# Two early blocks of a squared-ReLU feed-forward kernel put together: first products first, then seven quarter products over chunks 2 to 5

## The chip, the cores and the metric

The kernel runs on one core of one Trainium2 chip. The metric is the device time of one execution in microseconds (us); the kernel before took 207.84 us, the median of three runs (207.48 to 207.92). A core has five engines that each work off their own instruction stream in program order: TensorE (PE, matrix products, with its weight loads shown as PEld), VectorE (DVE), ScalarE (ACT), GpSimd (POOL) and SyncE (SP, here only an issuer of DMAs). An instruction that waits for another engine's result holds back everything behind it on its own engine.

## The reference

A retention recurrence with one decay per head, followed by a two-layer feed-forward with a squared ReLU:

```python
# q, k, v: (4, 8, 768, 64) fp32; w_in: (512, 2048); w_out: (2048, 512)
for t in range(S):
    state = gamma[None, :, None, None] * state + einsum('bhd,bhe->bhde', k[:, :, t], v[:, :, t])
    y[:, :, t] = scale * einsum('bhd,bhde->bhe', q[:, :, t], state)
x = y.transpose(0, 2, 1, 3).reshape(3072, 512)
h = maximum(x @ w_in, 0)
out = (h * h) @ w_out
```

The output is 3072 x 512 in fp32; the products are made in bf16.

## The kernel before, in words

**Tiles.** The 3072 tokens are 24 chunks of 128 (six to a batch entry). For each chunk an "attention" part makes `xt`, the transposed 512 x 128 input of the feed-forward: scale q and k (DVE), bring v to bf16 in `v_bd` (POOL), transpose q and k on PE and copy them out of PSUM (`qT`, `k_bd`, ACT), score products on PE (two halves, each with four 128-wide matmuls into the single PSUM buffer `st`), masking of each half into `pt` (DVE), a state product and its copy `s_bd`, the output products `y` (PE), and a copy of `y` into `xt` (ACT). Chunks 0 to 3 are done in pairs at the start, chunks 4 to 7 by `attend`, chunks 8 to 23 in a packed form by `attend2`, whose transposes are DMAs.

**Blocks.** The feed-forward goes over blocks of chunks, `BLOCKS = [4, 2, 2, ...]`: block 0 is chunks 0 to 3, block 1 chunks 4 and 5, block 2 chunks 6 and 7. The first product of a block (x @ w_in) fills a PSUM bank `psf` of 128 x 512 by four groups of matmuls or more; ACT takes it out with a ReLU into `h` (`relu`, L779) and DVE squares it in place (L750). Four `psf` banks rotate. The second product (h @ w_out) comes in two forms. Blocks 0 and 1 use the plain form (`second`, L966): 16 matmuls of 512 columns for a chunk, then ACT copies the bank to `osb` and SP stores it. Blocks 2 to 10 (`SEVEN`) use seven quarter products (`seven_products`, L785 to 901): the two chunks of a block and the two halves of w_out are taken as 2 x 2 blocks, and seven products of 8 matmuls with 256 columns (L804) take the place of eight; this needs sums of parts of `h` on DVE (`first_sums`, s3, s4, L800), and four sums of parts of w_out (`sum_w_out`, L303, 8 instructions in the whole kernel).

**Order.** The order of work is written out by hand. The feed-forward is cut into pieces, each about 0.87 us of PE work: 12 pieces for block 0's first product (one 128-row slice f = 4 to 15 of `h` each; f = 0 to 3 are done before), 16 for its second, 8 for block 1's first product, 8 for its second, and so on. After each piece a counter n goes up by one, starting with 5 after the first, and `before(n)` issues whatever was `put` at place n: parts of the attention of a later chunk, casts of weights, loads. Then `take_squares` issues the squares that are due. So a place is a position in every engine's stream. A pipeline step at place n stands on PE between piece n and piece n + 1.

**Around the change.** SP's stream starts with q, k, v of chunks 0 to 3, then the four quarters of w_in (1 MB each; each is cast to bf16 by DVE, ACT and POOL, `cast_w`), then q, k and v of chunk 4, then chunks 5, 6, 7 as their places come. POOL loads w_out with a cast in the DMA (`load_w_out`, L159) at places 7, 11, 15 and 19. Chunk 4's attention lies at places 21 to 31, chunk 5's at 28 to 35, chunk 6's at 30 to 42, chunk 7's at 40 to 49. At places 35 to 44 DVE clears ten parts of tiles for the packed form (`zero_off_diagonal`, L342). Pools that matter here: `stage` has 4 buffers (w_in's quarters, then k and v of whole batches), `opool` has 4 (`osb`), `ps_st` has 1.

Of the kernel before, what the change touches and what calls it, by code (L numbers as in the profile page):

```python
# [25 lines left out]


SEVEN = range(2, 11)
# [3 lines left out]
def kernel(  # L32
# [55 lines left out]
    def load_q(m):  # L88

        b, i = chunks[m]  # L90
        t = ldqpool.tile([P, H, 2, D], FP32, name="qn")
        src = q[b, :, i * C : (i + 2) * C, :].rearrange("h (s r) d -> s h r d", r=2)
        nc.sync.dma_start(t[:], src)
        raw_q[m] = t
# [11 lines left out]
    def load_kv(m):  # L106
        b, i = chunks[m]
        for name, src, to in (("kn", k, raw_k), ("vn", v, raw_v)):
            if m % 2 == 0:
                kv_tiles[name] = ldpool.tile([P, 2 * H * D], FP32, name=name)  # L110
            t = kv_tiles[name].rearrange("s (c h d) -> s c h d", c=2, h=H)[:, m % 2]
            nc.sync.dma_start(t, src[b, :, i * C : (i + 1) * C, :].rearrange("h s d -> s h d"))
            to[m] = t

    def load(m):
        if m % 2 == 0:
            load_q(m)
        load_kv(m)

    def stage_tile(size):  # L120
        t = stage.tile([P, 2 * NCH * NPAIR * D], FP32, name="stage")
        return t[:, 0:size]

    def batch_loads(m, name, size):
# [4 lines left out]
        t = stage_tile(2 * NCH * NPAIR * D)  # L129
# [38 lines left out]
    for g in range(1, NQ):  # L168
        load_w_in(g)
# [171 lines left out]
    def zero_off_diagonal(t, hh):  # L341
        nc.vector.memset(t[halves[hh], :, 1 - hh, :], 0.0)  # L342
# [12 lines left out]
    def scale_kv(m):  # L355
        b, i = chunks[m]
        ks = kspool.tile([P, H, D], BF16, name="ks")
        scale(nc.vector, ks, raw_k.pop(m), kf[:, i])
        v_bd = v_bds[m % 2]
# [4 lines left out]
        at[m].update(ks=ks, v_bd=v_bd)  # L364
# [378 lines left out]

    def take_squares():
        while squares:
            hv, on_scalar = squares.pop(0)
            if on_scalar:
                nc.scalar.activation(hv, hv, AF.Square)  # L748
            else:
                nc.vector.tensor_mul(hv, hv, hv)  # L750
# [27 lines left out]
    def relu(hv, hp, on_scalar=False):  # L778
        nc.scalar.activation(hv, hp[:], AF.Relu)  # L779
        squares.append((hv, on_scalar))  # L780
# [124 lines left out]
    def first_unit(tb, g, c, parts=(0, 1)):  # L905
# [11 lines left out]
        if 1 in parts:  # L917
            relu(h_of(tb, g * FPQ, (g + 1) * FPQ)[:, :, cols], open_ps.pop((tb, g, c)))

    def ffn_pieces(tb):  # L920
# [8 lines left out]
        elif tb <= 2:  # L929

            for c in range(nch):
                for g in range(NQ):
                    first_unit(tb, g, c)
                    if tb in SEVEN and (c, g) == (1, 3):
                        first_sums, rest = seven_products(tb)
                        first_sums(slice(0, 4))
                    yield
            if tb in SEVEN:
                yield from rest()
                return  # L940
        else:
            h_tiles(tb)
            per = 512 // TB
            if tb in SEVEN:
                first_sums, rest = seven_products(tb)
            for f0 in range(0, NFB, per):
# [3 lines left out]
                relu(h_of(tb, f0, f0 + per), hp, tb in SEVEN and f0 // per in (1, 3))  # L950
# [4 lines left out]
                if f0 // per == 5 and tb in SEVEN:  # L955
                    first_sums(slice(0, 4))
                yield
            if tb in SEVEN:
                yield from rest()
                return  # L960


        def second(op, j, g, cols=slice(0, DM)):
            for fq in range(FPQ):
                f = g * FPQ + fq
                nc.tensor.matmul(  # L966
                    op[:],
                    lhsT=h_of(tb, f)[:, 0, j * C : (j + 1) * C],
                    rhs=w_out_bf[g][:, fq, cols],
                    start=(f == 0),  # L970
                    stop=(f == NFB - 1),
                )

        def store(op, j, cols=slice(0, DM)):
            osb = opool.tile([P, DM], FP32, name="osb")
            nc.scalar.activation(osb[:, cols], op[:], AF.Copy)
            r0 = (first[tb] + j) * C
            nc.sync.dma_start(out[r0 : r0 + C, cols], osb[:, cols])


        together = nch if tb == 0 else 1
        for j0 in range(0, nch, together):
# [187 lines left out]
```

## Time and profile before

| | before |
|---|---|
| median of 3 runs | 207.84 us (207.48 to 207.92) |
| profiled execution, time | 208.11 us |
| its span, first to last instruction | 206.3 us |
| granted TensorE clock, mean over the span | 0.992 |
| PE / PEld / DVE / ACT / POOL busy | 197.0 / 160.4 / 151.4 / 132.5 / 64.3 us |
| ReLU of a 128 x 512 bank on ACT (L779) | 96 of 595 ns |
| square of 128 x 512 on DVE (L750) / on ACT (L748) | 80 of 475 ns / 16 of 630 ns |
| second product, plain, 512 columns (L966) | 96 matmuls |

How to read it: the profile is one execution, whose time outside the span is 208.11 - 206.3 = 1.8 us. Matmuls are pipelined and their listed length holds the time in the array, so the rate of PE is better read from the chain of waits, where eight matmuls in a row stand with the time that they add. Busy time of an engine counts no waits. In the timeline a row merges instructions of one kind that follow one another ("x8"), the first column is the start, the second the time from the start of the first to the end of the last, and brackets give idle time in front of the row and what ended it.

### The profile page before, as it was taken

The page shows a single profiled execution, that of the slowest core. Times are in us where ns is not written, and L with a number is a line of the kernel's source. Part 1 is how long each engine was busy: PE and PEld are TensorE (multiplying, and loading weights), DVE is VectorE, ACT ScalarE, POOL GpSimd, SP SyncE. Part 2 cuts the span into 40 slices and gives each one's busy share as a digit, 9 for nine tenths or more (in the row PEclk, how much of TensorE's full clock was granted, in tenths as well). Part 3 has the DMA queues.
Part 4 walks back from the last instruction along what each step waited for, and adds up shares of the span by engine and source line. Part 5 has one row for each costly group of instructions (what it writes and reads, how often), then busy time and mean ns, then how long its engine had stood idle before and what let it go on. Part 6 is the DMA issues. An engine that isn't in the chain of part 4 may idle for free.

```text
span 206.3 us, 5736 instructions
## 1 busy us (share of the span) xinstructions
PE 197.0 (95%) x2325; PEld 160.4 (78%) x2325; DVE 151.4 (73%) x304; ACT 132.5 (64%) x267; POOL 64.3 (31%) x122
## 2 busy tenths in 40 slices
PE   5698999999999999999999999999999999999993
PEld 1467644457975898988989999999988989998882
DVE  4777896538796899579588697797796797484373
ACT  8365884147945585792795794784776776864720
POOL 5332654011210441462245235252226226100000
PEclk9889999999999999999999999999999999999999
DMA  6999999999999978999999999998868952400202
GB/s 160 290 313 379 365 213 208 197 249 265 289 184 135 289 132 124 214 220 215 132 227 152 200 242 170 201 221 186 155 188 161 242 104 31 128 3 1 104 0 102
DMA packets 92730, 38.12 MB, mean 185 GB/s; under 512 B 68512, under 2 KB 88224, under 8 KB 92704
## 3 DMA queue, kind: packets, MB, share of 16 engines
q1 hardware_dynamic: 90592, 35.66, 82.2%
q0 software_dynamic: 2112, 2.10, 6.3%
q8 instruction: 18, 0.29, 0.7%
q14 instruction: 8, 0.07, 0.1%
HBM read 27.26 MB, written 6.29 MB: 163 GB/s over the span
## 4 chain that ended last, share of the span: by engine, by line
PE 79%; DVE 8%; ACT 5%; DMA 4%; issue 3%; POOL 0%; DVEq 0%
PE psf L770 36%; PE psf L804 13%; PE tp L804 9%; PE psf L966 8%; DMA qn<-in_q_dram 2%; DVE h L750 2%; DMA kT<-ks_bdp 2%; PE st L671 2%; PE y L727 2%; PE y L720 1%; PE c_ps L698 1%; ACT h L779 1%; ACT k_bd L395 1%; PE y L326 1%; DVE pt L558 1%
## 5 line engine op out<-in xcount | busy, mean ns | idle before, releaser
L770 PE MATMUL psf<-xt,w_in_bf 128*128 128x256 bf16 (+2 forms) x880 | 91.9, 259 | 0.2 <-ACT xt L498 0.2
L770 PEld LDWEIGHTS <-w_in_bf 128*128 128x128 bf16 x880 | 71.1, 98 | 11.6 <-issue 0.3
L779 ACT ACTIVATE h<-psf 128x512 bf16<-128x512 f32 x96 | 56.2, 595 | 17.3 <-PE psf L770 16.6
L750 DVE TENSOR_TENSOR h<-h 128x512 bf16<-128x512 bf16 x80 | 36.6, 475 | 16.1 <-ACT h L779 15.5
L632 POOL CAST ks_bdp<-stage 64x512 bf16<-64x512 f32 x32 | 24.9, 777 | 41.5 <-issue 24.4
L649 POOL COPY v_bd<-v 64x512 bf16<-64x512 bf16 x32 | 20.6, 644 | 39.1 <-DVE v L641 38.0
L804 PEld LDWEIGHTS <-h 128*128 128x128 bf16 x288 | 26.2, 98 | 4.0 <-DVE h L750 1.2
L800 DVE TENSOR_TENSOR osb<-psf,u 128x256 f32<-128x256 f32 x34 | 13.7, 422 | 17.2 <-ACT u L845 10.0
L966 PE MATMUL psf<-w_out_bf,h 128*128 128x512 bf16 x96 | 22.5, 379 | 0.0
L345 DVE TENSOR_TENSOR qs<-qn,qf 128x512 bf16<-128x512 f32 x22 | 17.7, 816 | 1.5 <-DMA qn<-in_q_dram 1.5
L734 ACT ACTIVATE xt<-y 128x512 bf16<-128x512 f32 x16 | 12.0, 747 | 8.8 <-PE y L727 8.8
L966 PEld LDWEIGHTS <-h 128*128 128x128 bf16 x96 | 8.9, 98 | 9.0
L804 PEld LDWEIGHTS <-k_bd 128*128 128x128 bf16 x144 | 13.8, 98 | 1.5
L707 ACT ACTIVATE s_bd<-c_ps 64x256 bf16<-64x256 f32 x29 | 10.6, 367 | 3.6 <-PE c_ps L698 3.6
L641 DVE TENSOR_TENSOR v<-stage,kf 128x512 bf16<-128x512 f32 x16 | 12.6, 786 | 0.0
L678 DVE TENSOR_TENSOR pt<-st,cmask 128x512 bf16<-128x512 f32 x16 | 11.0, 687 | 0.9 <-PE st L671 0.5
L804 PE MATMUL tp<-w_out_bf,h 128*128 128x256 bf16 x72 | 11.2, 273 | 0.2 <-DVE h L750 0.2
L708 ACT ACTIVATE s_bd<-c_ps 64x256 bf16<-64x256 f32 x29 | 11.0, 378 | 0.4
L800 DVE TENSOR_TENSOR k_bd<-h 128x512 bf16<-128x512 bf16 x18 | 10.7, 597 | 0.3
L421 DVE TENSOR_TENSOR pt<-st,cmask 128x512 bf16<-128x512 f32 x8 | 5.5, 689 | 7.4 <-PE st L414 7.4
L804 PE MATMUL psf<-w_sum,h 128*128 128x256 bf16 x72 | 10.8, 273 | 0.0
L748 ACT ACTIVATE h<-h 128x512 bf16<-128x512 bf16 x16 | 10.1, 630 | 0.5
(129 smaller groups left out, 277.5 us busy)
## 6 DMA issues: line engine op xcount, KB each, us to landing
qn<-in_q_dram SPq DMA_DIRECT2D x12, 512.0 KB, 5.1
out_dram<-osb SPq DMA_DIRECT2D x23, 256.0 KB, 3.5
stage<-in_moe_w_in_dram SPq DMA_DIRECT2D x3, 1024.0 KB, 11.9
stage<-in_k_dram SPq DMA_DIRECT2D x32, 96.0 KB, 4.1
stage<-in_v_dram SPq DMA_DIRECT2D x32, 96.0 KB, 4.0
w_out_bf<-in_moe_w_out_dram POOLq DMA_DIRECT2D x4, 512.0 KB, 10.5
kn<-in_k_dram SPq DMA_DIRECT2D x2, 512.0 KB, 6.4
vn<-in_v_dram SPq DMA_DIRECT2D x2, 512.0 KB, 7.2
```

Source lines behind the costliest of these rows:

```text
L345: engine.tensor_tensor(out=out, in0=by, in1=table[:, :, None].to_broadcast([P, H, D]), op=ALU.mult)
L632: nc.gpsimd.tensor_copy(ks[rows, :, hh, :].rearrange("s (u p) d -> s u p d", u=2), kn[rows])
L641: nc.vector.tensor_tensor(out=v2.rearrange("s (u p) d -> s u p d", u=2), in0=vn, in1=kf2[:, i, :, :, None].to_broadcast([P, 2, NPAIR, D]), ...
L649: nc.gpsimd.tensor_copy(v_bd[rows, :, hh, :], v2[rows])
L678: nc.vector.tensor_tensor(out=pt[:], in0=st[:], in1=cmask2.rearrange("s r t -> s (r t)")[:, None, :].to_broadcast([P, 2 * NPAIR, C // 2]), ...
L734: nc.scalar.activation(xts[tb][:, :, off : off + C].rearrange("e p (s r) -> e p r s", r=2), y[:], AF.Copy,)
L750: nc.vector.tensor_mul(hv, hv, hv)
L770: nc.tensor.matmul(hp, lhsT=w_in_bf[g][:, cb, fq * 128 : (fq + 1) * 128], rhs=xts[tb][:, cb, cols], start=(cb == 0), stop=(cb == NCB - 1),)
L779: nc.scalar.activation(hv, hp[:], AF.Relu)
L800: nc.vector.tensor_tensor(out=out, in0=in0, in1=in1, op=op)
L804: nc.tensor.matmul(to, lhsT=left[:, j], rhs=right(j) if callable(right) else right[:, j], start=(start and j == 0), stop=(stop and j == NF ...
L966: nc.tensor.matmul(op[:], lhsT=h_of(tb, f)[:, 0, j * C : (j + 1) * C], rhs=w_out_bf[g][:, fq, cols], start=(f == 0), stop=(f == NFB - 1),)
```

## The change

The first product of block 1 (chunks 4 and 5) is moved in front of block 0's second product. Chunks 0 and 1 keep the plain second product, as 8 pieces of four matmuls for two chunks in turn. Chunks 2 and 3 (called x below) and chunks 4 and 5 (y) get seven quarter products, interleaved by hand in one list (`early_pieces`, 112 matmuls of 256 columns, a piece for each 7 of them). The places are counted as before: 5 to 16 block 0's first product, 17 to 24 block 1's, 25 to 32 the plain product, 33 to 48 the seven products; from 49 on block 2 as before.

With it move: the attention of chunks 4 and 5 (places 8 to 19), 6 and 7 (31 to 44); the loads (q and k of chunk 4 in front of the last quarter of w_in, which is split in two; v of chunk 4 and k, v of chunk 5 behind it; chunks 6 and 7 as five DMAs from POOL's queue at place 20; w_out at 13, 14, 16, 17); the sums of w_out (25 to 31). Block 1's squares are held back and done on ACT at places 25 to 32. The sums of `h` for x (8 instructions of 512 columns, places 18 to 24) and for y (4 of 1024 columns, places 33 to 36) write a scratch tile from `stage`, which later becomes the tile of the k loads of chunk 12 on. The ten clears go to POOL.

```diff
-        nc.vector.memset(t[halves[hh], :, 1 - hh, :], 0.0)
+        nc.gpsimd.memset(t[halves[hh], :, 1 - hh, :], 0.0)
...
-    for g in range(1, NQ):
-        load_w_in(g)
+    load_w_in(1)
+    load_w_in(2)
+    load_q(4)
+    load_kv(4, "k")
+    load_w_in(3, parts=2)
+    load_kv(4, "v")
+    load_kv(5, "k")
+    load_kv(5, "v")
...
+    def late_square(on_scalar):
+        square(late_squares.pop(0)[0], on_scalar)
...
+        def p1(e):
+            e.oa, e.ob = (opool.tile([P, DM], FP32, name="osb") for _ in range(2))
+            yield from product(e, "pa", e.left(0, 0), w[0, 0], True)
+            copy(e.oa[:, lo], e.pa)
+        def p2(e):
+            yield from product(e, "pb", e.left(0, 1), w[1, 0], True)
+            add(e.oa[:, lo], e.pb)
+        def p6(e):
+            yield from product(e, "pa", of(e.s[1]), of(t2), False)
+            copy(e.oa[:, hi], e.pa)
+        def p5(e):
+            yield from product(e, "pd", of(e.s[0]), of(t1), True)
...
+        def c22(e):
+            add(e.ob[:, hi], e.pd)
+            nc.sync.dma_start(out[e.r0 + C : e.r0 + 2 * C], e.ob[:])
+            return ()
+        def p3(e):
+            yield from product(e, "pd", of(e.s[2]), w[1, 1], False)
+            add(e.oa[:, hi], e.pd)
+            nc.sync.dma_start(out[e.r0 : e.r0 + C], e.oa[:])
+        order = [
+            (p1, x), (p1, y), (p2, x), (p6, x), (p6, y), (p5, x), (p7, x), (p7, y), (p4, x),
+            (c22, x), (p4, y), (p3, x), (p5, y), (p2, y), (c22, y), (p3, y),
+        ]
...
+    def attend(m, q_at, qturn_at, k_at, v_at, turn_at, scores_at, state_at, outputs_at):
...
     put(6, cast_w, "in", 2)
-    for g, place in enumerate((7, 11, 15, 19)):
+    put(11, cast_w, "in", 3, (0,))
+    put(13, cast_w, "in", 3, (1,))
+    attend(4, (8, 9), 10, 9, 13, 11, (12, 13), 14, 15)
+    attend(5, None, None, 15, 17, 16, (17, 18), 18, 19)
+    for place, g in zip((13, 14, 16, 17), range(NQ)):
         put(place, load_w_out, g)
-    for m, place in ((5, 10), (6, 14), (7, 18)):
-        put(place, load, m)
-    put(10, cast_w, "in", 3)
-    for half, at_places in enumerate(((25, 25, 25, 25), (31, 31, 48, 48))):
+    put(20, load_q, 6, nc.gpsimd)
+    for m, name in ((6, "k"), (6, "v"), (7, "k"), (7, "v")):
+        put(20, load_kv, m, name, nc.gpsimd)
+    attend(6, (31, 32), 34, 32, 33, 35, (36, 37), 38, 40)
+    attend(7, None, None, 36, 38, 38, (40, 41), 41, 44)
+    early_at(0, 2, 0, 18, (18, 19, 20, 21, 21, 22, 23, 24))
+    for half, at_places in enumerate(((25, 25, 26, 26), (29, 30, 30, 31))):
...
-    attend(4, 21, (23, 25, 27, 29, 31))
-    attend(5, None, (28, 30, 32, 33, 35))
-    attend(6, 30, (33, 35, 37, 39, 42))
-    attend(7, None, (40, 42, 44, 46, 49))
+    for place in range(25, 33):
+        put(place, late_square, True)
+    early_at(1, 0, 3, 32, (33, 33, 34, 36))
     packed = pack_constants()
     put(27, next, packed)
     put(34, next, packed)
...
-        (12, "k"): [47, 48, 49, 50, 52, 53, 55, 56] + [74 + j for j in range(8)],
+        (12, "k"): [49, 50, 51, 52, 53, 54, 55, 56] + [74 + j for j in range(8)],
...
+    def pieces():
+        yield from first_pieces(0)
+        yield from first_pieces(1)
+        yield from plain_pieces(0, range(2))
+        yield from early_pieces((0, 1))
+        for tb in range(2, len(BLOCKS)):
+            yield from first_pieces(tb)
+            yield from rests[tb]()
```

In `early_pieces`, p7 and p4 are like p6 (bank `pa` goes on accumulating and is copied to a quarter of `ob` by ACT each time); p2, c22 and p3 add a bank onto the copied quarter on DVE (128 x 256). x and y have one bank each for `pa`, `pb` and `pd`. The arguments of `attend` are the places of: the two scalings of q, the transposes of q, the scaling of k, the cast of v, the transposes of k, the two score halves, the state, the outputs.

## The prediction

> **What bounds the kernel now.** I read the page's busy times and chain first, then PE's timeline in the stretch that changes, then ACT, DVE and POOL there.
>
> ```profile
> PE 197.0 (95%) x2325; PEld 160.4 (78%) x2325; DVE 151.4 (73%) x304; ACT 132.5 (64%) x267; POOL 64.3 (31%) x122
> ...
> PE 79%; DVE 8%; ACT 5%; DMA 4%; issue 3%; POOL 0%; DVEq 0%
> ```
>
> PE is busy for 95% of the span and has 79% of the chain. The slices behind the first four show a granted clock of 0.9 or more. So what counts is the work that PE does, and how long its stream stands still for another engine.
>
> ```profile
> 21.10 12.25 PE psf L770 x80
> ...
> 62.32 1.73 PE psf L966 x8
> ...
> 80.33 0.91 PE tp L804 x8
> 81.24 0.87 PE psf L804 x8
> ```
>
> The chain (start, length, what) gives PE's rates: 8 matmuls of 512 columns add 1.73 us (0.216 each), 8 of 256 columns 0.87 (0.109). The 12.25 us from 21.10 are 32 matmuls of 128 columns (1.78; 16 take 0.89 elsewhere in the chain) and the 12 pieces of block 0's first product: 10.47, or 0.8725 a piece. The first of them starts at 33.35 - 10.47 = 22.88.
>
> ```profile
> 49.81 1.05 PE L770 MATMUL psf<-xt,w_in_bf 128*128 128x128 bf16 x16 [0.19 <-ACT xt L498]
> ...
> 61.92 0.40 PE L388 MATMUL tp<-ident,ks 128*128 128x128 bf16 x4 [0.27 <-DVE ks L345]
> ```
>
> PE's timeline shows two of its few marked waits between 21 and 76 us, 0.19 and 0.27. All work from 22.88 to block 2's first product (68.30 in the chain) adds up to 44.35: 10.47 + 7.12 (8 pieces of block 1) + 96 x 0.2163 + 6.00 for the attention of chunks 4 to 7 without chunk 7's outputs (transposes of q 0.45, of k 0.22, a score half 0.22, state 0.22 to 0.24, outputs 0.66, chunk 6's 0.44). 68.30 - 22.88 - 44.35 = **1.07 us** in which PE stood still, marked or not.
>
> ```profile
> 27.34 0.60 ACT L779 ACTIVATE h<-psf 128x512 bf16<-128x512 f32 x1 [0.27 <-PE psf L770]
> 28.21 0.60 ACT L779 ACTIVATE h<-psf 128x512 bf16<-128x512 f32 x1 [0.27 <-PE psf L770]
> ...
> 51.57 1.02 ACT L381 ACTIVATE qT<-tp 128x1024 bf16<-128x1024 bf16 x1
> ...
> 54.64 1.19 ACT L395 ACTIVATE k_bd<-tp 64x512 bf16<-64x512 bf16 x2
> ```
>
> ACT's rows: beside block 0's first product it has a ReLU (0.60) for each piece of 0.87, so 0.27 us free in each. In before, the copy of q's transposes (1.02) and the two `k_bd` copies (1.19) lie beside the second product, which has no ReLU, or two or more pieces ahead of the scores that need them.
>
> **The saving.** 64 matmuls of 512 columns (13.85 us) go, 112 of 256 (12.21) come: **-1.6 us** on PE. With the old standing time gone as well, -1.07, the stretch from 22.88 to the start of block 2, now with chunk 7's outputs (0.66) inside it, would be 43.4 us instead of 46.1: -2.7 in all. Against this stand the places at which PE now waits. I worked each through in program order: an instruction starts when its engine is free and its inputs are there, with 0.1 us from PE to another engine and 0.05 back, as the chain's seams show.
>
> **1. Transposes of q, chunk 4 (place 10).** PE gets there after f = 9, at 28.1. DVE must first do, after the square of f = 6:
>
> ```profile
> 26.13 0.77 DVE L750 TENSOR_TENSOR h<-h 128x512 bf16<-128x512 bf16 x2
> ...
> 28.32 1.48 DVE L315 CAST w_in_bf<-stage 128x256 bf16<-128x256 f32 x4
> ...
> 80.33 0.68 DVE L800 TENSOR_TENSOR h<-h 128x1024 bf16<-128x1024 bf16 x1
> 80.93 0.69 DVE L800 TENSOR_TENSOR v_bd<-h,k_bd 128x1024 bf16<-128x1024 bf16 x1
> ```
>
> That square ends at 26.9 (first row). Then come scaling r = 0 (0.65, two take 1.30), the square of f = 7 (0.42), scaling r = 1 (0.65): 28.6. Wait 0.5 to 0.8; I take **0.6**.
>
> **2. First scores, chunk 4 (place 12).** From the end t of f = 9, ACT: qT starts at t + 0.6 + 0.45 + 0.1, ends at t + 2.17; ReLU of f = 10 to 2.77; w_in's part (0.36) to 3.13; two `k_bd` copies to 4.33. PE is there at t + 0.6 + 0.45 + 0.87 + 0.22 + 0.87 = t + 3.01. Wait **1.4**. One piece lies between transposes and scores, and ACT needs 2.2 us in it.
>
> **3. First scores, chunk 5 (place 17).** From the end of f = 15, ACT has its ReLU until 0.71 and `k_bd` until 1.91; PE is there at 0.22 + 0.89 = 1.11. Wait **0.85**.
>
> **4. First scores, chunk 6 (place 36).** Let T be the end of the plain product. ACT has two `osb` copies (0.60 each, at PE's ends T - 0.87 and T) with the last two late squares (0.63 each) behind them, in turn: the last square ends at T + 1.7. Only then can DVE make y's sums; the two rows at 80 us are such sums of 1024 columns, 0.61 apart. Three end at T + 3.57. Behind them on DVE stand the two small instructions for the constants (0.4), on which ACT's exponential at place 34 waits: T + 4.26. Behind that in ACT's stream: a copy of p1 y (0.38) and `k_bd`, to T + 5.85. PE is there at T + 28 x 0.109 + 0.45 + 0.22 = T + 3.72. Wait **2.15**. The copy of p1 y also needs the buffer of chunk 0's `osb`, whose store lands 3.7 to 5.3 us after its issue (the stores of 46 to 52 us): nothing to 0.9 more; I take 0.25.
>
> **5. Last product p3 y (place 47).** It goes on accumulating in the bank that c22 y reads, and that addition stands on DVE behind the addition of p2 y, which needs p2 y's last matmul. No PE work lies between: 0.1 + 2 x 0.4 + 0.05 = **0.95** (128 x 256 additions, 0.42 each in the page's group of L800).
>
> The other dependencies have room: p4 x needs ACT's copy of p7 x, but chunk 6's outputs, scores and p7 y lie between (1.7 us against 1.2); x's sums (8 x 0.43 on DVE) end about 11 us ahead of their first use; the late squares 1 to 6 find ACT idle beside the plain product.
>
> **Loads.**
>
> ```profile
> 23.92 0.92 POOL L313 CAST w_in_bf<-stage 128x256 bf16<-128x256 f32 x2 [0.97 <-DMA stage<-in_moe_w_in_dram]
> ...
> 27.45 2.23 POOL L159 DMA_DIRECT2D w_out_bf<-in_moe_w_out_dram  x3
> 33.48 0.61 POOL L361 CAST v_bd<-vn 128x512 bf16<-128x512 f32 x1 [3.80 <-DMA vn<-in_v_dram]
> ```
>
> POOL's timeline gives landings: w_in's third quarter at 23.9, the fourth (its cast follows at 26.7), v of chunk 4 at 33.5. On SP's queue 512 KB of q took 1.6 us and 256 KB of k 0.9 (issue plus time to landing: 28.3, 29.2). In front of w_in's last quarter they move its halves to about 28.2 and 29.6; f = 12 starts at 32.7, after waits 1 and 2, so that is hidden, and would cost 1:1 from 3 us later on. q of chunk 4 lands at about 25.7, needed by DVE at 26.9. On POOL w_out's issue now stands behind the casts of v, so it is sent from about 31 us; before, the four landed within 43 - 24.8 = 18 us with others beside them, so 49 at the latest, wanted from 46.8 (first) to 52 (last): 0 here, some 4 us if 12 us later than the 36 to 44 that I work with. Five loads leave SP (14.8 us of issue time there) for POOL, 0.75 us each by w_out's rows, perhaps 1.5 with twice the packets; POOL is idle there. SP then issues q and the first k of chunk 8 earlier, 0.75 MB beside w_out (some 3 us, inside the same room), and stops at chunk 0's store. The ten clears cost POOL some 3 us in an idle stretch and take 2.2 off DVE. Behind place 48 nothing changes; PE comes later there, so loads have more time: 0, with 0.5 to either side.
>
> The Trainium skill (page "SBUF — State Buffer", section "Who interferes with whom") says that DVE copies in a two-port mode lock GpSimd out, so that descriptors of POOL's DMAs aren't written. Here the row above has three w_out issues in 2.23 us beside DVE's four casts from 28.32: 0.74 each, no such lock. By the rule it would be rival B; the row decides.
>
> **Sum.** -1.6 - 1.07 + 0.6 + 1.4 + 0.85 + 2.15 + 0.25 + 0.95 = **+3.5 us**. The profiled span 206.3 becomes 209.8, its time 208.11 becomes 211.6; the median is 0.27 below that execution: **211.3 us**. The same steps on the kernel before give 0.5 + 0.2 + 0.7 = 1.4 us of waits where 1.07 were found, so they err by some 0.3.
>
> **Rivals.**
> **A, faster.** The three waits on `k_bd` don't come about, because ACT's short copies get done in the gaps. For it: in before, no marked PE wait names a `k_bd`. Against it: there two pieces lie between, here one, and ACT's stream is in order. Then 0.6 + 0.95 are left against -2.7: -1.1, 206.7. It decides when the five waits together stay under 2.7.
> **B, loads late.** The five loads on POOL's queue land 12 us after the 45 to 49 that I assume. For it: loads in before took up to 15 us to land while w_out ran. Against it: they follow w_out, and the need begins at 51. q of chunk 6 at 57 holds its transposes 3.7 us and adds 0.4 to wait 4: 215.4. It decides from 8 us late on.
> **C, half the waits.** The waits are there, but wait 4 is shortened, since the exponential or y's sums come earlier than my order says (ACT alone would make it 1.2), and 1 and 2 merge into 1.2: -2, 209.3.
> That the saving is not made can be left out: products of 256 columns already run at 0.109 here.
>
> **How the numbers follow.** Forecast 0.62 (its own range 210.0 to 212.8), A 0.10, B 0.13, C 0.15. The range 208.2 to 214.4 leaves out A and somewhat over half of B, 0.18. A measurement of this kernel tells 0.2% (0.4 us) from no change: faster 0.09, within it 0.03, slower 0.88.
>
> **What would show it.** In the new profile: PE idle ahead of chunk 4's and chunk 5's first scores, released by ACT's `k_bd` copies, about 1.4 and 0.85; the longest ahead of chunk 6's first scores, about 2.2, with ACT's exponential waiting for DVE just before; 0.95 ahead of the last quarter product, for a DVE addition; block 2's first product starting about 72.4. I am wrong if PE runs through these without gaps, or if it waits there for a DMA.

## The result, and the profile after

| | before | after |
|---|---|---|
| median of the runs | 207.88 us (207.48 to 208.03) | 213.11 us (212.35 to 214.22) |
| ratio, 95% interval | | 1.0259 (1.0202 to 1.0316) |
| profiled execution: time, span | 208.11, 206.34 | 212.47, 210.56 |
| block 2's first product, chunk 7's outputs ahead of it | 68.80 | 72.67 |
| from there to the start of the last addition into `osb` | 134.14 | 133.97 |
| from there to the end of the span | 3.40 | 3.92 |

Before, block 2's first product stands at 68.14 in PE's timeline, and 0.66 us are added for the outputs of chunk 7, which followed later there. So the profiled execution lost 3.87 us ahead of block 2, won 0.17 behind it, and lost 0.52 after the last sum; 0.14 more lie outside the span. The page's lines for the engines and for the chain (first busy time, share, instructions; then shares of the chain):

```profile
PE 197.1 (94%) x2370; PEld 165.0 (78%) x2373; DVE 151.9 (72%) x304; ACT 137.2 (65%) x279; POOL 73.6 (35%) x137
...
PE 68%; DMA 9%; DVE 8%; ACT 6%; SPq 6%; issue 1%; DVEq 0%
```

PE is listed as busy for the same time as before (197.0), with 45 more and shorter instructions; the lengths overlap, so this line does not show whether work was saved, and the rates in the chain have to. The chain has moved from PE (79 to 68%) to DMA, SP and ACT. Where PE stands is in its timeline; these are all its marked rows between 29 and 73 us (start, length, engine, line, operation; in brackets idle time and what ended it):

```profile
29.99 0.38 PE L393 MATMUL tp<-ident,ks 128*128 128x128 bf16 x4 [0.25 <-ACT qT L386]
...
31.87 0.34 PE L419 MATMUL st<-qT,k_bd 128*128 128x128 bf16 x3 [0.39 <-ACT k_bd L400]
...
34.87 0.82 PE L782 MATMUL psf<-xt,w_in_bf 128*128 128x512 bf16 x3 [0.20 <-DVE w_in_bf L317]
...
39.01 0.34 PE L419 MATMUL st<-qT,k_bd 128*128 128x128 bf16 x3 [0.38 <-ACT k_bd L400]
...
56.65 0.38 PE L393 MATMUL tp<-ident,ks 128*128 128x128 bf16 x4 [0.35 <-DVE stage L1019]
...
58.63 0.23 PE L419 MATMUL st<-qT,k_bd 128*128 128x128 bf16 x1 [0.83 <-ACT k_bd L400]
59.25 0.34 PE L419 MATMUL st<-qT,k_bd 128*128 128x128 bf16 x3 [0.39 <-ACT k_bd L400]
...
71.80 1.03 PE L1068 MATMUL psf<-w_out_bf,stage 128*128 128x256 bf16 x8 [0.85 <-DVE osb L1079]
```

Five of the eight name ACT's `k_bd` copies (L400) or the DVE addition to `osb` (L1079), as forecast; the other three were not: DVE's cast of w_in, and twice k's transposes, which wait for ACT's copy of q's (L386; at 56.65 a sum on DVE that ends with that copy is named, and the variants name the copy). A bracket is shorter than the time that PE loses, since the listed length of the row before it runs on after the last matmul was sent. So I measured a loss from the start of one row to the start of the next, less the row's matmuls at the rates of the chain; for the last row that gives 1.01 instead of 0.85. Some rows lack the record of a matmul whose weight load is there (three at 32.05 where the piece has four, for one); these are counted in full. The chain of the same place (start, length, what) shows where block 2 begins and the last wait in front of it:

```profile
71.33 0.42 DVE osb L1079
71.76 0.04 issue
71.80 1.03 PE psf L1068 x8
72.83 2.68 PE psf L782 x48
```

ACT, from the end of the plain second product:

```profile
52.74 0.60 ACT L989 ACTIVATE osb<-psf 128x512 f32<-128x512 f32 x1 [2.34 <-PE psf L980]
53.23 0.62 ACT L751 ACTIVATE h<-h 128x512 bf16<-128x512 bf16 x1
53.75 0.59 ACT L989 ACTIVATE osb<-psf 128x512 f32<-128x512 f32 x1
54.23 0.63 ACT L751 ACTIVATE h<-h 128x512 bf16<-128x512 bf16 x1
...
55.58 1.02 ACT L386 ACTIVATE qT<-tp 128x1024 bf16<-128x1024 bf16 x1 [0.45 <-PE tp L380]
57.59 0.24 ACT L267 ACTIVATE kf<-ex_k_f 128x48 f32<-128x48 f32 x1 [0.99 <-DVE ex_k_f L186]
...
58.00 1.19 ACT L400 ACTIVATE k_bd<-tp 64x512 bf16<-64x512 bf16 x2
```

The last late square ends at 54.86, the exponential waits 0.99 for DVE (`ex_k_f`), and only then come the two `k_bd` copies, to 59.19. The DVE rows that belong to it:

```profile
33.19 1.63 DVE L317 CAST w_in_bf<-stage 128x256 bf16<-128x256 f32 x2
...
54.89 0.69 DVE L1019 TENSOR_TENSOR stage<-h 128x1024 bf16<-128x1024 bf16 x1 [1.03 <-ACT h L751]
55.62 0.99 DVE L1019 TENSOR_TENSOR stage<-stage,h 128x1024 bf16<-128x1024 bf16 x1
56.53 0.68 DVE L1019 TENSOR_TENSOR h<-h 128x1024 bf16<-128x1024 bf16 x1
57.13 0.18 DVE L185 CAST ex_k_f<-ex_k_i 128x48 f32<-128x48 int32 x1
57.35 0.21 DVE L186 TENSOR_TENSOR ex_k_f<-ex_k_f,lng 128x48 f32<-128x48 f32 x1
```

y's first sum waits 1.03 for that square, the constants' two small instructions stand behind three sums: wait 4, link by link. The cast in the first row takes 0.82 a piece; I come back to it. GpSimd's loads:

```profile
31.61 2.43 POOL L155 DMA_DIRECT2D w_out_bf<-in_moe_w_out_dram  x3
...
35.29 0.93 POOL L90 DMA_DIRECT2D qn<-in_q_dram  x1
...
41.78 0.89 POOL L109 DMA_DIRECT2D vn<-in_v_dram  x1 [2.91 <-DMA w_out_bf<-in_moe_w_out_dram]
...
53.34 0.98 POOL L366 CAST v_bd<-vn 128x512 bf16<-128x512 f32 x1 [8.29 <-DMA vn<-in_v_dram]
```

The loads of chunks 6 and 7 are issued from 35.29 to 42.67, the last of them held 2.91 us by w_out. v of chunk 6 is there at 53.34; from 45 to 49 was assumed.

### The profile page after: what moved, and what is told of

The parts are those of the page before. It is cut to its first block, busy times and chain, and to the rows that moved or that the text cites. A ratio compares the mean times of both kernels' runs of the same rounds, so it can differ in the third digit from the quotient of the medians.

```text
span 210.6 us, 5857 instructions
## 1 busy us (share of the span) xinstructions
PE 197.1 (94%) x2370; PEld 165.0 (78%) x2373; DVE 151.9 (72%) x304; ACT 137.2 (65%) x279; POOL 73.6 (35%) x137
## 4 chain that ended last, share of the span: by engine, by line
PE 68%; DMA 9%; DVE 8%; ACT 6%; SPq 6%; issue 1%; DVEq 0%
PE psf L782 32%; PE psf L816 13%; PE tp L816 9%; DMA stage<-in_moe_w_in_dram 5%; PE psf L980 3%; SPq L98 3%; PE psf L1068 2%; DMA kT<-ks_bdp 2%; DMA qn<-in_q_dram 2%; DVE h L753 2%; ACT h L791 2%; PE st L676 2%; PE y L732 2%; ACT k_bd L400 2%; DVE w_in_bf L317 1%; PE y L725 1%
## 5 line engine op out<-in xcount | busy, mean ns | idle before, releaser
L753 DVE TENSOR_TENSOR h<-h 128x512 bf16<-128x512 bf16 x72 | 32.3, 464 | 14.8 <-ACT h L791 14.5
L816 PEld LDWEIGHTS <-h 128*128 128x128 bf16 x288 | 26.3, 98 | 3.7 <-DVE h L753 0.9
L751 ACT ACTIVATE h<-h 128x512 bf16<-128x512 bf16 x24 | 14.5, 626 | 0.5
L816 PE MATMUL psf<-w_sum,k_bd 128*128 128x256 bf16 x80 | 10.4, 273 | 0.0
L732 PE MATMUL y<-pt,v_bd 128*128 128x64 bf16 x128 | 9.4, 193 | 0.0
```

The source lines that it names most:

```text
L732: nc.tensor.matmul(yv, lhsT=a["v_bd"][:, u * NPAIR + p], rhs=a["pt"][:, u * NPAIR + p, :].rearrange("s (r t) -> s r t", r=2), start=not inter,
L816: nc.tensor.matmul(to, lhsT=left[:, j], rhs=right(j) if callable(right) else right[:, j], start=(start and j == 0), stop=(stop and j == NF ...
```

## The experiments

Every kernel is the changed one with the edit shown. "Block 2 at" is the start of its first product in PE's timeline (after: 72.67); "the rest" is from there to the start of the last addition into `osb` (after: 133.97). Ratios are against the kernel before in the same series, whose median was between 207.49 and 207.84 us. The stretch itself begins (with the piece f = 4) at 22.83 before and at 22.80 after, but between 22.50 and 23.48 in the variants, with nothing edited ahead of it. So small differences in "Block 2 at" are given from the start of f = 4 as well.

### The five waits, one by one

**The addition of c22 y a product earlier.**

```diff
-            (c22, x), (p4, y), (p3, x), (p5, y), (p2, y), (c22, y), (p3, y),
+            (c22, x), (p4, y), (p3, x), (p5, y), (c22, y), (p2, y), (p3, y),
```

> c22 y is put in front of p2 y. Theory (the last quarter product waits for an addition that stands on DVE behind another one): the 1.0 us of standing time ahead of p3 y goes, block 2's first product starts at 71.8 instead of 72.8, time 212.1 against 213.1 for the changed kernel. Rival (DVE is late there in any case): no change, 213.1.

212.93 us (212.25 to 213.51), ratio 1.0247 (1.0212 to 1.0282). PE's timeline of this kernel, at block 2's start and at one later place:

```profile
71.44 2.84 PE L782 MATMUL psf<-xt,w_in_bf 128*128 128x128 bf16 x48
...
118.12 0.41 PE L676 MATMUL st<-qT,kT 128*128 128x64 bf16 x8 [0.75 <-DMA kT<-ks_bdp]
```

Block 2 starts 1.23 us earlier (1.13 from f = 4), without a wait ahead of the last product: wait 5 was real and cost 1.0. The time hardly moved, because the rest took 135.33 us, 1.36 more: PE waits there for `kT`, the transpose that a DMA makes (1.4 us by the waits between 75 and 140, after: 0.2).

**The constants' exponential later.**

```diff
-    put(34, next, packed)
+    put(39, next, packed)
```

> The exponential of the packed constants goes from place 34 to 39. Theory (it holds ACT's stream until DVE has made y's sums, and the k_bd copies of chunk 6 stand behind it): chunk 6's first scores begin about 1.0 us earlier, time 212.1. Rival (the osb copies and late squares alone hold the k_bd copies): under 0.3 us gained, 212.8 or more.

211.81 us (211.54 to 214.22), ratio 1.0215 (1.0157 to 1.0274). PE's timeline at the first scores of chunk 6:

```profile
57.50 0.23 PE L419 MATMUL st<-qT,k_bd 128*128 128x128 bf16 x1
58.12 0.34 PE L419 MATMUL st<-qT,k_bd 128*128 128x128 bf16 x3 [0.39 <-ACT k_bd L400]
```

They start at 57.50 instead of 58.63 and have no wait in front; the 0.39 between the two `k_bd` halves stays. Block 2 at 71.90, 0.77 earlier (0.52 from f = 4): 0.36 of what was won is lost again ahead of chunk 7's scores. That the exponential held the `k_bd` copies is shown; the links ahead of it (square, three sums, constants) are read from the rows above. The ranges of the runs overlap with those of the changed kernel, so the time does not show it.

**Chunk 4's and 5's scores one piece further from their transposes.**

```diff
-    attend(4, (8, 9), 10, 9, 13, 11, (12, 13), 14, 15)
-    attend(5, None, None, 15, 17, 16, (17, 18), 18, 19)
+    attend(4, (8, 9), 10, 9, 13, 11, (13, 14), 14, 15)
+    attend(5, None, None, 14, 17, 15, (17, 18), 18, 19)
```

> Chunk 4's scores go to places 13 and 14, chunk 5's k scaling and transposes to 14 and 15, so that two pieces lie between transposes and scores. Theory (PE waits for ACT's k_bd copies only because one piece is too short for them): the waits of 0.75 and 0.6 ahead of the two first scores go, -1.2, time 211.9. Rival (ACT has more work than the stretch holds, the wait moves to the next thing that needs ACT, such as xt for block 1): no change, 213.1.

212.91 us (212.00 to 214.26), ratio 1.0248 (1.0194 to 1.0301). PE's waits from 22 to 75 us (what, us in total, times, longest), and a row of DVE's timeline:

```profile
PE st L419 <- DVE pt L426: 1.8, 2, 1.6
PE st L419 <- ACT k_bd L400: 1.5, 2, 1.1
```

```profile
32.88 1.35 DVE L317 CAST w_in_bf<-stage 128x256 bf16<-128x256 f32 x2
```

The waits on `k_bd` ahead of chunk 4's and chunk 5's scores (0.39 and 0.38 marked) are gone; the 1.5 that is left is chunk 6's (1.2 after). So one piece between transposes and scores was what made them. But a new wait of 1.6 comes: the second half of chunk 4's scores needs the buffer that DVE's `pt` reads, and `pt` now stands behind the casts of w_in, which take 1.35 us here. Block 2 at 73.50, 0.8 later: moved by one piece, the wait met the next one, as the rival had it, though on DVE and not on ACT.

**The late squares two to a piece, y's first sum earlier.**

```diff
-        put(place, late_square, True)
-    early_at(1, 0, 3, 32, (33, 33, 34, 36))
+        put(25 + (place - 25) // 2, late_square, True)
+    early_at(1, 0, 3, 28, (28, 31, 32, 33))
```

> Late squares two to a place at 25 to 28, y's sums at 28, 31, 32, 33. Theory (the last two squares stand behind the osb copies, and the sums, the exponential and chunk 6's k_bd copies behind them): the wait ahead of chunk 6's first scores falls from 1.55 to about 0.4, time 212.0. Rival (the sums are held by the sums of w_out, whose DMA lands at 49.4, and end no earlier): no change, 213.1.

214.93 us (214.58 to 216.29), ratio 1.0352 (1.0314 to 1.0389). DVE's timeline and a line of PE's waits from 22 to 76 us:

```profile
50.86 0.69 DVE L1019 TENSOR_TENSOR stage<-h 128x1024 bf16<-128x1024 bf16 x1 [4.94 <-ACT h L751]
51.47 0.68 DVE L305 TENSOR_TENSOR w_sum<-w_out_bf 128x1024 bf16<-128x1024 bf16 x1
```

```profile
PE tp L380 <- DVE qs L347: 1.9, 1, 1.9
```

y's first sum, now ahead of the last w_out sums in DVE's order, waits 4.94 us for a square, and all behind it with it: q's scaling comes 1.9 us too late for PE's transposes. Block 2 at 74.85. The cure for one wait of DVE put a longer one into its queue.

**w_out's loads behind both casts of v.**

```diff
-    for place, g in zip((13, 14, 16, 17), range(NQ)):
+    for place, g in zip((17, 17, 17, 17), range(NQ)):
```

> All four loads of w_out stand at place 17, behind both casts of v on POOL. Theory (DVE's two casts of w_in's last part took 1.1 to 1.7 us in five runs because POOL was issuing w_out's DMAs): they take 0.7 or less, and PE's 0.35 ahead of f = 14 goes; w_out lands some 3 us later, its first sum on DVE starts near 47. Rival (the casts are slow for another reason): 1.1 or more again.

One run, 213.42 us. The same casts of w_in, in DVE's timeline:

```profile
33.01 0.91 DVE L317 CAST w_in_bf<-stage 128x256 bf16<-128x256 f32 x2
```

GpSimd sends nothing until 33.72 here, the two casts take 0.91 instead of 1.63 (between theory and rival), and the wait ahead of f = 14 is gone. Block 2 comes at 73.67 all the same, 1.0 later. That is PE's clock: from 59.14 to 62.55 the granted clock is 0.5 (1.0 around it), and a matmul of 256 columns takes 0.213 us there instead of 0.109. The same seven matmuls here and in the changed kernel:

```profile
60.77 1.70 PE L1068 MATMUL psf<-w_sum,stage 128*128 128x256 bf16 x7
```

```profile
60.59 0.93 PE L1068 MATMUL psf<-w_sum,stage 128*128 128x256 bf16 x7
```

Ahead of it chunk 6's scores start 0.43 earlier than in the changed kernel, behind it chunk 7's transposes 0.99 later, and from these to block 2 both take 11.0. So this run does not show what the edit is worth in time.

### What gives it back behind block 2

**The sums' tile kept apart from chunk 12's loads, these earlier** (with the edit of c22 y).

```diff
-            kept_tiles[12, "k"] = t
...
-        (12, "k"): [49, 50, 51, 52, 53, 54, 55, 56] + [74 + j for j in range(8)],
+        (12, "k"): [41, 42, 43, 43, 44, 44, 45, 45] + [74 + j for j in range(8)],
```

> As the run with c22 y in front, and the scratch tile is no longer kept for the k loads of chunk 12 on: these take the free slot of stage, at places 41 to 45. Theory (SP's stream is held at places 48 and 49 by p3 y's store and by the loads that wait for the scratch tile, so the transposes of k behind them come late): PE's waits for kT between 75 and 140 us, 1.4 in that run, go; time 211.6 against 212.9. Rival (those transposes are late because of POOL's casts or a full DMA): the waits stay over 1.0, time 212.9.

216.94 us (216.09 to 218.45), ratio 1.0417 (1.0373 to 1.0462). SP's timeline and PE's:

```profile
69.74 2.74 SPq L132 DMA_DIRECT2D stage<-in_k_dram  x4
...
76.46 1.33 SPq L660 DMA_TRANSPOSE kT<-ks_bdp  x1
```

```profile
80.53 0.41 PE L676 MATMUL st<-qT,kT 128*128 128x64 bf16 x8 [4.66 <-DMA kT<-ks_bdp]
```

The eight loads stand in SP's order ahead of chunk 8's `kT`, which goes out at 76.46 instead of 70.12, and PE waits 4.66 us for it. From 81.12 to 84.53, just behind this wait, the granted clock is 0.5. The same 32 matmuls here and in the changed kernel, where the clock stays at 1.0:

```profile
80.77 3.29 PE L782 MATMUL psf<-xt,w_in_bf 128*128 128x128 bf16 x32
```

```profile
76.59 1.95 PE L782 MATMUL psf<-xt,w_in_bf 128*128 128x128 bf16 x32
```

From chunk 8's scores to chunk 9's it is 7.45 us instead of 5.82. So the rest, 5.2 longer than in e1_c22_first, is 3.7 of waits on `kT` and 1.6 of clock; neither theory nor rival had the waits grow. What makes the clock fall is not shown; the edit is not a test of it. What had filled SP's order up to there stands further up; SP's waits in the changed kernel, 20 to 90 us:

```profile
SPq L991 <- ACT osb L989: 20.7, 1, 20.7
```

SP stops 20.7 us at chunk 0's store, so 14 of chunk 8's 16 loads go out only from 53.8 to 65.1.

**All waits attacked at once:** the edits of e5_k12_own_slot and e2_exp_late, and these (the last one splits the `k_bd` copies of chunks 4 and 5 between ACT and DVE).

```diff
-        put(place, late_square, True)
-    early_at(1, 0, 3, 32, (33, 33, 34, 36))
+        put(25 + (place - 25) // 2, late_square, True)
+    early_at(1, 0, 3, 32, (32, 33, 33, 36))
...
-    put(13, cast_w, "in", 3, (1,))
+    put(12, cast_w, "in", 3, (1,))
...
-        put(turn_at, transpose_k, m)
+        put(turn_at, transpose_k, m, ps_tp, "tp", m < 6)
```

> All edits at once: c22 y in front; exponential at 39; late squares two to a place with y's sums at 32 to 36; the last cast of w_in at 12; half of the k_bd copies of chunks 4 and 5 on DVE; k of chunk 12 in its own slot. Theory (the time went into these waits one by one): -1.0 - 2.0 - 0.35 - 1.2 from 213.1, 208.6. Rival (ACT, DVE and the loads are full there, so that waits move rather than go): 211 or more.

216.81 us (216.56 to 216.92), ratio 1.0423 (1.0391 to 1.0455). Block 2 at 70.90, 1.77 earlier than after (1.46 from f = 4) and still 2.1 later than before; the rest 140.2, with 4.6 us of waits on `kT` and, behind the longest of them (79.23 to 82.65), again a clock of 0.5 that costs 1.6. The rival holds: of 5.5 us of waits ahead of block 2 some 1.5 went, and more came back behind it.

**The same without the early loads.**

```diff
+            kept_tiles[12, "k"] = t
...
-        (12, "k"): [41, 42, 43, 43, 44, 44, 45, 45] + [74 + j for j in range(8)],
+        (12, "k"): [49, 50, 51, 52, 53, 54, 55, 56] + [74 + j for j in range(8)],
```

> The five edits of the run with all waits taken away, but the loads of chunk 12's keys stay where the changed kernel has them (places 49 to 56, in the tile that held the sums). Theory (the waits on TensorE ahead of block 2 are one part of the loss, the transposes kT that stand in SyncE's order the other, and the early loads of chunk 12 alone made the second part large): block 2's first product at 70.9 +- 0.4 as in that run, from there to the last osb sum 134.0 to 135.3 as in the changed kernel and its first variants, and 5.8 around it: 210.7 to 212.0 us, waits of TensorE on kT 0.2 to 1.4 us. Rival (whatever starts block 2 earlier is given back on kT, since the loads behind chunk 0's store are not earlier): waits on kT at least 2 us and 212.5 to 214 us.

211.70 us (211.30 to 213.06), ratio 1.0205 (1.0178 to 1.0231): 5.1 us of the last kernel's loss were the early loads, by way of the wait and the clock behind it. Block 2 at 71.42, 0.1 outside what was expected (f = 4 starts at 23.43, 0.9 later than in e7_all_waits; from there it is 1.88 less than in the changed kernel), the rest 135.58, 0.3 outside, in the profiled execution (212.72 us, the second longest of six). PE's waits there, 75 to 140 us:

```profile
PE st L676 <- DMA kT<-ks_bdp: 1.5, 3, 0.7
```

Of the 1.25 us won ahead of block 2 all is lost behind it in that execution (+1.61). The median is 1.4 below that of the changed kernel, with intervals that overlap. The time is the theory's; the waits on `kT`, 1.5, lie just above its 1.4 and below the rival's 2.

**The stores of chunks 0 and 1 from ScalarE's queue,** alone and together with the last edit.

```diff
                     r0 = (first[tb] + j) * C
-                    nc.sync.dma_start(out[r0 : r0 + C], osb[:])
+                    nc.scalar.dma_start(out[r0 : r0 + C], osb[:])
```

> The changed kernel, but the two stores of the plain second products (chunks 0 and 1) are issued from ScalarE's queue, behind the copy that they wait for, and not from SyncE's. Theory (SyncE standing 20.7 us for chunk 0's osb pushes chunk 8's loads together with the transposes, and that makes the waits on kT of 0.2 to 1.4 us that differ from run to run): the row of 20.7 us is gone, the loads of chunk 8 are issued before 50, kT of chunk 8 is at SyncE by 70 without a load behind it, waits on kT after 72 at most 0.2 us; block 2's first product stays at 72.6 +- 0.4: 212.0 to 212.5 us, and the runs lie within 0.6 us of one another, where those of the changed kernel lie 1.9 apart. Rival 1 (the waits on kT come from the DMA engines or from SyncE's later loads): 212.3 to 214.3 us with the same spread. Rival 2 (the earlier loads of chunk 8 crowd w_out and the loads of chunks 6 and 7, which land 2 us later): the first product of block 2 after 73.5 and 213.5 us or more.

> Both edits together: the waits taken away without the early loads of chunk 12, and the stores of chunks 0 and 1 from ScalarE's queue. Theory: block 2's first product at 70.9 +- 0.4, 133.6 to 134.0 from there, no waits on kT: 210.3 to 210.8 us, still 1.2 % slower than the kernel before, because the stretch ahead of block 2 stays 2 us longer. Rival (the waits on kT do not hang on chunk 0's store): as the run without the store's move, 210.7 to 212.0 us, or more.

Alone 215.48 us (214.51 to 215.97), ratio 1.0378 (1.0356 to 1.0401); together 213.00 (212.16 to 214.23), 1.0259 (1.0231 to 1.0288). SP's and DVE's timeline of the first:

```profile
30.54 19.00 SPq L132 DMA_DIRECT2D stage<-in_k_dram  x8
49.66 14.27 SPq L132 DMA_DIRECT2D stage<-in_v_dram  x8
```

```profile
51.71 0.69 DVE L305 TENSOR_TENSOR w_sum<-w_out_bf 128x1024 bf16<-128x1024 bf16 x1 [4.20 <-DMA w_out_bf<-in_moe_w_out_dram]
```

The stop of 20.7 us is gone and chunk 8's loads do start at 30.54, but eight of them take 19.00 us to go out, beside w_out and the loads of chunks 6 and 7 (0.65 each when they go out from 53.77 in the changed kernel). w_out's second half is there at 51.71 instead of 49.43, the sums and the exponential come later, and block 2 at 75.66: rival 2. Only about half of these 3.0 us are the loads', though: chunk 6's scores start 1.44 later than in the changed kernel, and the other 1.5 have come by 65.57, with a granted clock of 0.5 from 62.06 to 65.48. By that estimate block 2 would come at about 74.1 without it, still inside rival 2. The mean clock of the four other executions, 0.982 to 0.984, is no higher than this one's (0.987). The stop at chunk 0's store kept these loads apart from w_out's. In the second kernel, whose clock stays at 1.0 in this stretch, block 2 comes at 72.25 (71.42 without the move), and the waits on `kT` stay, 1.6 us. So they do not hang on that store.

**Chunk 12's first eight loads from GpSimd's queue** (with the edits of e9_waits_without_slot).

```diff
                 for p in range(NPAIR):
-                    nc.sync.dma_start(
+                    queue = nc.gpsimd if (m, name, w) == (12, "k", 0) else nc.sync
+                    queue.dma_start(
```

> The run e9_waits_without_slot, but the first eight loads of chunk 12's keys (places 49 to 56) are issued from GpSimd's queue and not from SyncE's. Theory (SyncE issues without a pause from 71 to 120, with 12 transposes behind loads in its order, so that a block 2 that starts earlier only meets the same kT times: 83.1, 89.1, 95.6 in both; eight issues of 0.65 us fewer, 5.2 us, take that bound away): kT of the third to fifth chunk issued at 78 to 82, 84 to 88 and 91 to 95, waits of TensorE on kT after 75 at most 0.2 us instead of 1.5, block 2's first product at 71.4 +- 0.4, 134.0 to 134.5 from there to the last osb sum, 210.9 to 211.4 us. Rival 1 (the waits on kT come from the transposes' own time in the DMA engines, 1.3 or 2.0 to 2.9 us by what else moves, and not from SyncE's order): kT issued earlier, but waits of 1 us and more stay, 211.5 to 212.7 us. Rival 2 (GpSimd stands at place 49 until the sums' tile is free and keeps v_bd and ks_bdp of chunk 9 waiting): a wait on ks_bdp or v_bd of over 0.5 us on TensorE, or kT of chunk 9 at SyncE later than 76.5, and 212 to 214 us.

212.19 us (210.91 to 213.61), ratio 1.0216 (1.0189 to 1.0243), not faster than with SP. A line of SP's waits from 70 to 125 us and one of PE's from 75 to 140:

```profile
SPq L661 <- POOL ks_bdp L638: 10.4, 6, 4.8
```

```profile
PE st L677 <- DMA kT<-ks_bdp: 2.4, 3, 0.8
```

SP has time now, 10.4 us of it spent on waiting for GpSimd's casts, and PE waits for `kT` all the same, 2.4 us. The early `kT`s go out at 82.70, 88.59 and 95.86, as in the kernel that it was made from (83.05, 89.11, 95.58). The theory falls: those eight loads are not what holds `kT`. Waits and time are those of rival 1, but its earlier `kT`s did not come either.

### One part of the change alone

**The reordering without quarter products in chunks 2 to 5** (their sums go too; all other places stay as they are).

```diff
-    early_at(0, 2, 0, 18, (18, 19, 20, 21, 21, 22, 23, 24))
...
-    early_at(1, 0, 3, 32, (33, 33, 34, 36))
...
-        yield from early_pieces((0, 1))
+        yield from plain_pieces(0, range(2, 4))
+        yield from plain_pieces(1, range(2))
```

> The order and places of the changed kernel, but chunks 2 to 5 with the plain second product and no sums for them. Theory (the crowded attention of chunks 4 and 5 costs most, the seven products give 1.7 and cost 1.0 ahead of p3 y and about 1.0 through y's sums): 213.1 + 1.7 - 2.0 = 212.8. Rival (the seven products with their sums are what costs, the new order costs nothing): 208 to 209.

211.15 us (210.84 to 211.54), ratio 1.0154 (1.0120 to 1.0187). All of PE's waits that are listed from 22 to 76 us:

```profile
PE st L419 <- ACT k_bd L400: 1.1, 3, 0.4
PE tp L393 <- ACT qT L386: 0.5, 2, 0.2
```

Block 2 at 71.56 (0.83 earlier than after from f = 4), the rest 133.57, no wait on `kT`. Against before the reordering costs 3.3 us in the median. Against this kernel the quarter products cost 2.0 more, though they save 1.64 us of PE's work: the exponential no longer waits for DVE here, no `k_bd` wait is over 0.4, and there is no p3 y to wait for. The truth lay between theory and rival, nearer to the theory.

## Why the prediction came out as it did

The direction, the mechanism ahead of block 2 and the wide range were right; 211.3 was 1.8 us short of 213.11, which lies 0.3 above the forecast's own range (210.0 to 212.8). The wide range holds it only because its upper end was set for a part of rival B, which did not come. About half of the 1.8 us is in the profiled execution, 212.47 instead of 211.6: 0.37 more ahead of block 2, 0.17 less behind it, 0.52 after the last sum and 0.14 outside the span. The other half is that the median lies 0.64 above that execution, where 0.27 below it was taken. The steps against what PE's timeline of the changed kernel shows, in us:

| step | forecast | measured | where |
|---|---|---|---|
| work saved | -1.64 | -1.64 | 96 x 0.2163 becomes 32 x 0.2163 and 112 x 0.109 |
| old standing time gone | -1.07 | -1.07 | all standing time of the stretch is listed below |
| 1, q's transposes | 0.6 | 0.3 | between the two halves, at 28.48 |
| 2, chunk 4's scores | 1.4 | 1.2 | 0.41 ahead of k's transposes, 0.17 + 0.56 + 0.08 in the scores |
| 3, chunk 5's scores | 0.85 | 0.75 | 0.21 + 0.54 |
| 4, chunk 6's scores, store | 2.4 | 2.25 | 0.51 ahead of k's transposes, 0.99 + 0.56 + 0.19 in the scores |
| 5, last product | 0.95 | 1.0 | ahead of p3 y |
| not foreseen | 0 | 0.35 + 0.2 + 0.5 | cast of w_in ahead of f = 14; chunk 7's scores; gaps under 0.15 |
| sum | +3.5 | +3.85 | block 2: +3.87 |

- **The waits.** As a sum the five came to 5.5 instead of 6.2. That +3.5 met +3.87 so closely is partly luck: waits that were 0.7 too long stood against 1.05 that were not foreseen. Two of them have another shape than I gave them: 0.41 and 0.51 of waits 2 and 4 lie ahead of k's transposes, which share one PSUM buffer with q's and wait for ACT's copy of those. I had let them start at once and put the whole delay in front of the scores. The totals are 0.15 to 0.2 below the forecast, since ACT's stream decides both places.
- **The saving** was made, and was paid for by the waits that only the quarter products bring: e8_plain_products has 1.64 us more of PE work and starts block 2 1.1 us earlier (0.8 from f = 4).
- **The cast ahead of f = 14.** I had f = 14 free of waits, with 0.36 for half of the w_in part on ACT and DVE's casts at the 0.37 a piece of the row before. They took 0.82 a piece beside a w_out issue and a cast of v on GpSimd. 0.35 us.
- **Loads.** Those of chunks 6 and 7 landed at 51.2 to 55 us, some 6 us later than assumed, and not the 8 from which rival B would decide. PE has no wait in this stretch that names a DMA. "Hidden" was right, with less room than I said.
- **Rivals A and C** fell: the `k_bd` waits are there, and wait 4 came out long by the order that I gave, with the exponential waiting for DVE. In one half C was near: waits 1 and 2 came to 1.5, where it said 1.2 and the forecast 2.0.
- **Behind place 48: 0, with 0.5 to either side.** This is the mis-sized term. In the profiled execution it holds (-0.17), but 0.5 us come after the last sum (below), and the other three runs took 212.35, 213.75 and 214.22. The clock does not sort these: the two shorter runs have a mean granted clock of 0.990 and 0.991, the two longer ones 0.992 and 0.999. Profiles of the variants differ in the same way behind block 2, and where the rest is long, PE waits for `kT` (75 to 140 us):

| run | rest | waits on `kT` |
|---|---|---|
| e8_plain_products | 133.57 | 0 |
| e6_w_out_late | 133.90 | 0 |
| e4_squares_early | 133.92 | 0.2 |
| changed kernel | 133.97 | 0.2 |
| e10_stores_on_scalar_queue | 134.05 | 0.3 |
| e2_exp_late | 134.46 | 0.7 |
| e3_scores_apart | 134.94 | 1.1 |
| e1_c22_first | 135.33 | 1.4 |
| e9_waits_without_slot | 135.58 | 1.5 |
| e11_waits_and_stores | 135.62 | 1.6 |
| e12_k12_on_pool | 136.46 | 2.4 |

Less these waits the rest is 133.6 to 134.1 in every row; e5_k12_own_slot and e7_all_waits join them when the 1.6 us of clock are taken off as well. That this makes up the spread of the changed kernel's own runs is argued from these; the longer ones have no profile.

**What stays open** is why `kT` comes late. Two places have most of the waits.

- The scores of chunk 14, at 117 to 119 us, where e1_c22_first, e9_waits_without_slot, e11_waits_and_stores and e12_k12_on_pool wait. Their `kT` is issued 4.0 us ahead of them in the changed kernel, 3.4 in these four (in e2_exp_late and e3_scores_apart too, without a marked wait), and 5.3 in e8_plain_products (4.7 before, at 109.88). From the `kT` at about 96 to this one SP needs 18.3 us in the changed kernel, 18.9 to 19.8 in those six, 16.9 in e8_plain_products and 17.6 before. Between them stand a `kT`, a `qT` and 18 loads and stores; a load's issue takes 0.6 us, but the longest 1.3 to 2.5, except in e8_plain_products (0.65).
- The scores of chunk 16, at 132 to 140 us, where the changed kernel and all variants but e6_w_out_late and e8_plain_products wait, 0.2 to 1.1 us. Here the transfer itself is longer: from issue to landing this `kT` takes 4.2 to 5.0 us where PE waits, 4.0 before and in e6_w_out_late, 3.4 in e8_plain_products.

So a stretch won ahead of block 2 is not kept by SP there. What makes SP's issues and this transfer longer was not found: neither chunk 0's store nor chunk 12's first loads.

No version beat the kernel before: the nearest, e8_plain_products, is 1.5% slower, and the best with quarter products, e9_waits_without_slot, e2_exp_late and e12_k12_on_pool, 2.0 to 2.2%.

## What to carry to other kernels

Moving matmuls between two chains is free only if the engines that feed them have the same room at the new place: here PE's own work fell by 1.6 us, and ACT's 0.27 us per piece, which had been plenty two pieces ahead, was too little one piece ahead. Before such a move, write down each feeding engine's order with its row durations; this gave four of the five waits to 0.2 us and the first to 0.3. And count what the freed time does to the queue behind it: 1.2 us won ahead of block 2 was lost again, in one profile wholly, on a DMA transpose in another engine's queue. And read the granted clock beside the waits before a longer stretch is put down to an edit: in four variants 3.4 us at half clock cost about 1.5 us.

## What was not expected of the hardware

- **Casts of f32 to bf16 on DVE beside GpSimd.** A 128x256 cast takes 0.28 us by itself (four in a row 0.89, at 25.05, with GpSimd waiting). Beside GpSimd's work some take much longer: 0.96 and 0.74 at 33.19 and 34.07 in the changed kernel, 0.61 and 0.81 in e3_scores_apart, one of two 0.70 in e6_w_out_late, and two of four 0.54 and 0.62 at 28.32 in the kernel before. Each of these ends 0.11 to 0.16 us after the end of the GpSimd instruction beside it, be it a w_out issue or a cast of v. So the 0.37 a piece on which the forecast built is a mean of free and held casts. The forecast had weighed this for GpSimd; it was DVE that was slower. The Trainium skill (page "SBUF — State Buffer", section "Who interferes with whom") says that of two instructions that need the shared port pair the one that issues first has it and the other blocks; the slow casts agree with that, but the first at 28.32 ran in 0.29 us inside an issue begun before it, and no run here separates the port from other causes.
- **GpSimd's DMA issues are not all alike.** 0.76 to 0.81 us for 512 KB of w_out, 0.89 to 0.93 for q, k and v of 256 to 512 KB, and one stood 2.91 us until a w_out load had landed.
- **The end of the span.** From the end of the last addition to the end of the span it took 3.10 us before, 3.6 to 3.7 in the changed kernel and in ten of its variants, and 4.15 and 4.19 in the two in which ScalarE's queue is used too. So 0.5 us of this change lie behind the last instruction that does work. The last store lands 2.1 us after that addition both before and after; the rest are closing instructions that the timeline does not list, and why they take longer is not shown.
- **A half clock in the middle of a kernel.** In e5_k12_own_slot, e6_w_out_late, e7_all_waits and e10_stores_on_scalar_queue the granted clock is 0.5 for 3.41 us inside the stretches compared here, and matmuls take twice as long. The comparison of before and after is free of it: there it stands at 8.6 to 12.0 and at 8.5 to 11.9, ahead of the stretch in both. In e5_k12_own_slot and e7_all_waits it begins 0.6 and 0.3 us behind a wait of over 4 us; in e6_w_out_late and e10_stores_on_scalar_queue there was no wait as long, and in e4_squares_early a wait of 1.9 us brought none.
